# Attention with beacon keys and a low-rank mixer on one core: masks built ahead of the key loads, one q load put off, the score order of the first pair, the first mixing two blocks side by side, and the first second layer taken by halves of w2

## The chip, the core and the metric

The kernel runs on one core of one Trainium2 chip. The core has five engines that run their own instruction streams and meet through semaphores: TensorE (matrix multiply, PE in the profile; its weight loads are shown as PEld), VectorE (DVE), ScalarE (ACT), GpSimd (POOL) and SyncE (SP). Matmul results go to PSUM, which has eight banks; everything else lies in SBUF. Transfers are issued by SP, ACT or POOL and run on 16 DMA engines. The metric is the device time of the program in microseconds; a kernel's time is the median of its runs.

## The reference

Per batch (8) and head (8), causal attention over 576 tokens of width 64 with 16 beacon keys ahead of them, which every query sees. The eight heads side by side give x (576 x 512). Then a mixer: u = x + (U V applied along the tokens, rank 32), and out = u + relu(u w_ch1) w_ch2 with 512 -> 2048 -> 512.

```python
k_all = np.concatenate([beacon_k, k], axis=2)
v_all = np.concatenate([beacon_v, v], axis=2)
scores = scale * np.matmul(q, k_all.transpose(0, 1, 3, 2))
scores = np.where(causal, -1000000000.0, scores)
a = np.exp(scores - scores.max(-1, keepdims=True))
a /= a.sum(-1, keepdims=True) + 1e-09
x = np.matmul(a, v_all)                 # heads side by side
h = x.transpose(0, 2, 1) @ U @ V
u = x + h.transpose(0, 2, 1)
out = u + np.maximum(u @ w_ch1, 0.0) @ w_ch2
```

## The kernel before

**Tiling.** A pair is two heads (four pairs for each batch; pair p belongs to batch p // 4). Keys with beacons are cut into five tiles of 128 (the last shorter), queries likewise. The scores of a pair are computed with the keys on the partitions, in four groups of a PSUM bank each (`groups`; group g starts with key tile g), for both heads: 8 matmul results. ACT takes the exponential of each into `expt`, VectorE clears the masked part there (`mask_head`, L324, L326), and the weighted sums (`av_unit`, L397) use `expt` as the stationary side against v with a column of ones, so that the sum of weights comes out beside the result. For pairs 0, 1 and 4 the mask is instead added to the scores on TensorE before the exponential (`early`, L340), from `negmask`.

**Operands.** q and k of a pair are loaded with tokens on partitions, regrouped so that two heads lie side by side (`regroup`, L268, and L270 for the beacons), turned by TensorE (L275; L281 where nothing was regrouped) and copied to qT and kT (L308, L313). For pair 0 and for the q of pair 1 the loads stand in float32 in `first` (tiles `stk`, `stq`), issued by SP and ACT in `load_first` (L203); all other loads are issued by POOL, which casts to float16 in the transfer. Of pairs 0 and 1 regrouping is also the cast: for pair 0 one half is done by VectorE and the other by ACT.

**Constants.** `build_masks` makes the identity, `mask`, `bigmask` and `negmask` on POOL and VectorE. `small_loads` brings U and V (L167 to L172); its `cast` writes Usb and Vsb on POOL (L176, L177) and then copies V into the other partition groups of `Vsb` and `Vend` by transfers on SP (L181, L182). w_ch1 is loaded in four pieces (`emit_w1`, L189), w_ch2 in two halves (`emit_w2`, L195), all by POOL, between the loads of batch 0 and 1 and ahead of those of batch 2 (`load_batch(2)`).

**The order of the work.** It is written out by hand: within each engine instructions run in the order in which the program issues them. `queue` holds units of the mixer's two layers: `g_unit(dc)` is four matmuls of the first layer (L534) and a relu on ACT or VectorE (L547, L549); `c_unit(i, part)` is a quarter (four of 16 slices of the hidden width, L560) of output tile i of 128 rows. After part 3 u is added, the tile is copied to `ob` (L573 for later blocks; for the first block u is added on TensorE, L568, and the copy is VectorE's for even i, L577, and ACT's for odd i, L575) and stored by SP (L579). `fill(n)` takes n units out of the queue, and "f" in the lines of `play` is one. "q5" and "k5" turn q and k of pair 5, "r7" regroups, "v8:01" computes groups 0 and 1 of pair 8 (`visit`, L382), "a" and "b" are the two weighted sums.

Batch 0 is mixed in two halves of two 128-wide blocks each (`first_mix`): `head` multiplies U with x (L489), `begin` turns x onto PSUM (L413), `rest` adds the product with V (L506) and copies to uT. Batch 1 is mixed by `mix_units` (L434 to L476), whose pieces stand between units of the queue. After that come the lines

```python
        mix(1)
        fill(8)
        regroup_of(NP1)
        regroup_of(NP1 + 1)
        fill(8)
        play("q8 f k8 f v8:01 f q9 f k9 f r10 v8:23,9:0 f")
```

with NP1 = 8, so that the first operands of batch 2 are regrouped amid units of the first block's second layer. These are held in the order of `for i ... for part`. The queue at `mix(1)` is: the head, one unit, `most`, three units, `end`, and then units with empty places between, up to four of them; so the first `fill(8)` plays the head, units 0 to 3 with `most` and `end`, and unit 4; the second plays units 5 to 8.

PSUM banks are handed out in the order in which the program releases them (`pst`, `emptying`).

Of the kernel before, what the change touches and what calls it, by code (L numbers as in the profile page):

```python
# [11 lines left out]
F32 = mybir.dt.float32  # L12
# [6 lines left out]
P = 128  # L19
F16_MAX = 65504.0  # L20
# [10 lines left out]
def kernel(  # L31
# [13 lines left out]
    nc = tc.nc  # L45
# [76 lines left out]
    def build_masks():  # L122
        make_identity(nc, ident)
        nc.vector.memset(bigmask[:, 0, P - Nb : P], F16_MAX)
        nc.vector.tensor_copy(out=identb, in_=ident)
        token_load(nc.gpsimd, k[0], Ls[0][0][0], SETS[1])
        make_upper_triangular(nc, mask, val=F16_MAX, diag=True)
        prs[0] = [None, regroup(first, 0, 1, V, act_copy)]
        nc.vector.tensor_copy(out=bigmask[:, 0, 0 : P - Nb], in_=mask[:, Nb:P])
        nc.vector.tensor_copy(out=bigmask[:, 1, :], in_=mask)  # L130
        for i in range(2):
            nc.vector.tensor_scalar(
                out=negmask[:, i, :], in0=bigmask[:, i, :], scalar1=1.0, scalar2=NEG,
                op0=ALU.is_lt, op1=ALU.mult,
            )

    def clear():
        for c in range(2, 4):
# [23 lines left out]
    def small_loads():  # L162

        f = utp.tile([P, NT * R + S], F32, name="small", tag="ut")
        nc.vector.memset(f[0:1, 0:1], 0.0)
        uf, vf = f[:, 0 : NT * R].rearrange("p (j r) -> p j r", r=R), f[0:R, NT * R :]
        nc.sync.dma_start(out=uf[: nq[0], 0, :], in_=moe_U[0 : nq[0], :])  # L167
        nc.sync.dma_start(
            out=uf[:, 1 : NT - 1, :], in_=moe_U[q0[1] : QM, :].rearrange("(j p) r -> p j r", p=P)
        )  # L170
        nc.sync.dma_start(out=uf[:NL, NT - 1, :], in_=moe_U[QM:S, :])
        nc.sync.dma_start(out=vf, in_=moe_V)  # L172

        def cast():
            for rr, jj in ((nq[0], slice(0, 1)), (P, slice(1, NT - 1)), (NL, slice(NT - 1, NT))):
                nc.gpsimd.tensor_copy(out=Usb[:rr, jj, :], in_=uf[:rr, jj, :])  # L176
            nc.gpsimd.tensor_copy(out=Vsb[0:R, :], in_=vf)  # L177
            for cc in range(NCC):
                rs = ds(R * cc, R)
                if cc:  # L180
                    nc.sync.dma_start(out=Vsb[rs, :], in_=Vsb[0:R, :])  # L181
                nc.sync.dma_start(out=Vend[rs, cc, :], in_=Vsb[0:R, QM:S])  # L182

        return cast

# [16 lines left out]
    def token_load(eng, src, dst, hs):  # L202
        eng.dma_start(out=dst[0:TP, hs, :], in_=src[hs].rearrange("h (p j) d -> p h (j d)", j=TJ))  # L203
# [116 lines left out]
    def score_units(c, qT, kT, ex, early=False):  # L320

        def mask_head(i):
            e4 = ex[i][:, 0:EW].rearrange("p (g w) -> p g w", w=SLOT)[:, :, 0:P]
            nc.vector.tensor_tensor(out=e4, in0=e4, in1=bigmask, op=ALU.min)  # L324
            o, n = blk[(4, 4)], nq[4]
            nc.vector.tensor_tensor(  # L326
                out=ex[i][0:n, ds(o, n)], in0=ex[i][0:n, ds(o, n)], in1=mask[0:n, 0:n], op=ALU.min
            )

        def visit(gs, idle=0, by_head=True, between=None):  # L330
            turn = [(g, i) for i in range(2) for g in gs] if by_head else [(g, i) for g in gs for i in range(2)]
# [12 lines left out]
            for g in gs:  # L344
                for ch, qa, w, o in groups[g]:
                    for i in range(2):
                        hp = slice(D * i, D * i + D)
                        nc.tensor.matmul(  # L348
                            ps[g, i][:, ds(o, w)], kT[hp, c, ds(P * ch, P)], qT[hp, c, ds(qa, w)],
                            start=not early, stop=True, skip_group_check=early,  # L350
                        )

            def exps(g, i):
                nc.scalar.activation(  # L354
                    out=ex[i][:, ds(SLOT * g, gw[g])], in_=ps[g, i][:, 0 : gw[g]], func=AF.Exp, scale=scale
                )
# [11 lines left out]
        return [  # L368
            lambda idle=0, between=None: visit([0, 1], idle, between=between),
            lambda gs=[2, 3], by_head=True: visit(gs, 0, by_head), masks, mask_head,  # L370
        ]

# [108 lines left out]
    def first_mix(xb):  # L481

        qts = outp.tile([P, DM], F16, name="qfirst", tag="ob")
        cell = {}

        def head(c0, n):
            qtp = pst([R, P * n], F32, name="qtp")
            for j in range(NT):
                nc.tensor.matmul(  # L489
                    qtp, Usb[: nq[j], j, :], xb[: nq[j], j, ds(P * c0, P * n)], start=(j == 0), stop=(j == NT - 1)  # L490
                )
            nc.vector.tensor_copy(out=qts[0:R, ds(P * c0, P * n)], in_=qtp)
            emptying(qtp)

        def begin(c0, cs, n=2):
            for cc in cs:
                cell[cc] = pst([P, QM], F32, name="ups")
                x_into(xb, cell[cc], cc, list(range(NT - 1)), 0, True)
                if cc == c0:
                    cell["end"] = pst([P, n, NL], F32, name="uend")  # L500
                x_into(xb, cell["end"][:, cc - c0, :], cc, [NT - 1], QM, cc == c0)

        def rest(c0, n, copies, end):
            for at in (0, QM):
                for i in range(n):
                    nc.tensor.matmul(  # L506
                        cell["end"][:, i, :] if at else cell[c0 + i], qts[0:R, ts(c0 + i, P)],
                        Vsb[0:R, at : S if at else QM], start=False, stop=True, skip_group_check=True,
                    )
            for cc, copy in zip(range(c0, c0 + n), copies):  # L510
                copy(out=uT[:, cc, 0:QM], in_=cell[cc])
                emptying(cell[cc])
            end(out=uT[:, ds(c0, n), QM:S], in_=cell["end"])
            emptying(cell["end"])

        return head, begin, rest

    def mlp_units(t0, n, dst, flip, turned=True, last=False):
# [35 lines left out]
        def c_unit(i, part):  # L554
            m = min(P, n - P * i)
            if part == 0:
                cps["t"] = pst([P, DM], F32, name="cps")
            ps = cps["t"]
            for dc in range(4 * part, 4 * part + 4):
                nc.tensor.matmul(  # L560
                    ps[:m, :], gT["t"][:, dc, ds(P * i, m)], w2[:, dc, :], start=(dc == 0),
# [31 lines left out]
                nc.sync.dma_start(out=dst(i, P)[:, hs], in_=ob)  # L593

        units += [lambda dc=dc: g_unit(dc) for dc in range(NDC)]
        for i in range((n + P - 1) // P):
            c = c_half if last and i == n // P - 1 else c_unit
            units += [lambda i=i, part=part, c=c: c(i, part) for part in range(4)]
        return units, g_part


# [66 lines left out]
    def load_first():  # L668

        kf = gtp.tile([P, 2, TJ * D], F32, name="stk", tag="gT")  # L670
        qf = gtp.tile([P, 4, TJ * D], F32, name="stq", tag="gT")
        first.extend([kf, qf])
        for src, dst in ((q[0], qf), (k[0], kf)):
            for eng, h in ((nc.sync, 0), (nc.scalar, 1)):
                token_load(eng, src, dst, slice(h, h + 1))
        token_load(nc.sync, q[0], qf, SETS[1])
        Ls[0] = qk_tiles()
        key_beacons(nc.gpsimd, beacon_k[0], Ls[0][0][0], ALLH)
        nc.scalar.activation(out=warm, in_=ones, func=AF.Exp)
# [128 lines left out]
    with tc.manual_schedule(engines={ENG.PE, ENG.Activation, ENG.DVE, ENG.SP, ENG.Pool}):  # L808
# [11 lines left out]
        t0[0]()  # L820
        idle(IDLE[4], ident)
        t0[1]()
        sc[0](IDLE[1])
        prs[1] = [None, regroup(first, 1, 1, V)]
        for u in qkT_of(1)[::-1]:
            u()
        clear()
        cast = small_loads()
# [50 lines left out]
        rest(0, 2, (act_copy, act_copy), act_copy)  # L879
        av = av_of(3)  # L880
        av[0]()
        av[1]()
        begin(2, (2,))
        part(D0, 2)
        part(D1, 2)
        head(2, 2)
# [230 lines left out]
```

## Time and profile before

| | us |
|---|---|
| median of 3 runs | 350.42 (349.91 to 350.76) |
| profiled execution, device time | 350.22 |
| its span, first to last instruction | 348.6 |
| TensorE busy | 341.6 (98%) |
| VectorE busy | 190.5 (55%) |
| ACT busy | 163.5 (47%) |
| POOL busy | 98.0 (28%) |

All times in the views are counted from the start of the span. A row of a timeline has start, duration, engine, source line, operation, output and inputs, shape, the number of like instructions merged into it and, in brackets, how long the engine sat idle before it and what ended that. A matmul's end is modelled, so starts are the better measure of TensorE. A row of the chain of waits has start, length and the work that the end was waiting for at that time. A row of windows has the stretch, its length, the busy time and count of PE, PEld, DVE, ACT and POOL, the granted TensorE clock as a share of full speed, the DMA share and the bytes moved in GB/s. A row of DMA issues has output and input, queue, count, KB each and the median time from issue to landing. "SPq" and "POOLq" are the engines' instruction queues, where transfers are issued.

### The profile page before, as it was taken

How to read it: one execution, taken by the hardware profiler on the slowest of the kernel's cores; microseconds unless marked ns; L12 is line 12 of the kernel's file. 1: busy time of each engine (PE TensorE's matmuls, PEld its weight loads, DVE VectorE, ACT ScalarE, POOL GpSimd, SP SyncE). 2: the span in 40 equal slices, each digit the busy share in tenths (PEclk: the TensorE clock that was granted, in tenths of full speed). 3: DMA queues.
4: the chain of work that ended last, by engine and by line, in shares of the span. 5: the costliest groups of instructions: out<-in, count | busy, mean ns of one | idle time of the engine just before them, and what ended most of it. 6: DMA issues, size and time to landing. Idle time of an engine off the chain costs nothing.

```text
span 348.6 us, 7792 instructions
## 1 busy us (share of the span) xinstructions
PE 341.6 (98%) x3084; PEld 173.0 (50%) x3084; DVE 190.5 (55%) x492; ACT 163.5 (47%) x358; POOL 98.0 (28%) x137
## 2 busy tenths in 40 slices
PE   8999999999999999999999999999999999999995
PEld 3565564555554455444554545445445444444443
DVE  5776964789875653654565456535655542323311
ACT  5957851578823665167614753494434203302300
POOL 8885713653505547303830140000000000000000
PEclk9999999999999999999999999999999999999999
DMA  9999999999999999991999799613123314013011
GB/s 168 128 181 182 157 196 181 222 145 144 131 147 144 159 152 127 172 190 8 141 134 192 124 107 132 179 44 68 63 75 47 68 63 120 2 60 105 17 65 65
DMA packets 146635, 41.88 MB, mean 120 GB/s; under 512 B 131488, under 2 KB 142080, under 8 KB 146592
## 3 DMA queue, kind: packets, MB, share of 16 engines
q0 software_dynamic: 87440, 18.18, 71.6%
q1 hardware_dynamic: 58928, 22.84, 36.3%
q8 instruction: 26, 0.43, 0.6%
q10 hardware_dynamic: 224, 0.30, 0.3%
q14 instruction: 17, 0.14, 0.2%
HBM read 37.37 MB, written 9.44 MB: 134 GB/s over the span
## 4 chain that ended last, share of the span: by engine, by line
PE 88%; DMA 7%; DVE 2%; ACT 1%; issue 0%; POOL 0%
PE gps L534 35%; PE cps L560 33%; PE po L397 8%; PE sps L382 6%; DMA st<-in_q_dram 6%; ACT expt L354 1%; PE tps L275 1%; PE sps L348 1%; PE cph L586 1%; DMA stq<-in_q_dram 1%; PE qtp L434 1%; PE tps L281 1%; DVE qT L308 1%; DVE pr L268 1%; PE ups L459 1%; DVE kT L308 0%
## 5 line engine op out<-in xcount | busy, mean ns | idle before, releaser
L534 PE MATMUL gps<-uT,w 128*128 128x512 f16 x576 | 136.0, 379 | 0.1
L560 PE MATMUL cps<-w,gT 128*128 128x512 f16 x560 | 130.9, 379 | 0.1
L388 ACT ACTIVATE expt<-sps 128x496 f16<-128x496 f32 x192 | 82.5, 534 | 71.6 <-PE sps L382 71.6
L547 ACT ACTIVATE gT<-gps 128x512 f16<-128x512 f32 x86 | 50.9, 622 | 78.8 <-PE gps L534 78.7
L534 PEld LDWEIGHTS <-w 128*128 128x128 f16 x576 | 51.8, 98 | 58.0 <-issue 2.4
L560 PEld LDWEIGHTS <-gT 128*128 128x128 f16 x560 | 50.9, 98 | 59.4 <-issue 6.5
L549 DVE TENSOR_SCALAR gT<-gps 128x512 f16<-128x512 f32 x58 | 39.9, 690 | 41.6 <-PE gps L534 39.9
L573 DVE TENSOR_TENSOR ob<-cps,ut 128x512 f32<-128x512 f32 x31 | 21.4, 691 | 48.3 <-PE cps L560 47.5
L218 POOL DMA_DIRECT2D vs<-in_v_dram x50 | 39.6, 807 | 17.0 <-PE po L397 4.8
L397 PEld LDWEIGHTS <-expt 128*128 128x128 f16 (+1 forms) x960 | 36.2, 98 | 12.8 <-issue 1.0
L397 PE MATMUL po<-vs,expt 128*128 128x65 f16 (+1 forms) x960 | 38.9, 194 | 0.1
L406 DVE TENSOR_TENSOR xb<-po,rec 128x320 f16<-128x320 f32 x64 | 31.5, 491 | 2.2
L324 DVE TENSOR_TENSOR expt<-expt,bigmask 128x512 f16<-128x512 f16 x58 | 24.3, 418 | 6.7 <-ACT expt L388 6.7
L354 ACT ACTIVATE expt<-sps 128x496 f16<-128x496 f32 (+1 forms) x64 | 27.0, 606 | 0.7 <-PE sps L348 0.6
L405 DVE RECIPROCAL rec<-po 128x5 f32<-128x5 f32 x64 | 12.1, 188 | 26.9 <-PE po L397 26.6
L382 PE MATMUL sps<-qT,kT 64*128 64x80 f16 (+4 forms) x288 | 23.3, 281 | 0.1
L200 POOL DMA_DIRECT2D vs<-in_beacon_v_dram x8 | 4.3, 536 | 57.2 <-PE po L397 57.2
L646 POOL DMA_DIRECT2D st<-in_q_dram x20 | 16.9, 863 | 7.2 <-DMA vs<-in_v_dram 4.3
L382 PEld LDWEIGHTS <-kT 64*128 64x128 f16 x288 | 9.8, 94 | 18.3 <-issue 14.4
L646 POOL DMA_DIRECT2D st<-in_k_dram x20 | 16.9, 868 | 3.3 <-DMA st<-in_q_dram 2.9
L446 DVE TENSOR_TENSOR uT<-ups,uT 128x496 f16<-128x496 f32 x24 | 14.5, 667 | 5.0 <-PE ups L459 5.0
L308 DVE COPY qT<-tps 128x576 f16<-128x576 f16 (+1 forms) x16 | 11.8, 735 | 3.5 <-PE tps L281 2.3
(97 smaller groups left out, 162.4 us busy)
## 6 DMA issues: line engine op xcount, KB each, us to landing
out_dram<-ob SPq DMA_DIRECT2D x35, 256.0 KB, 2.3
vs<-in_v_dram POOLq DMA_DIRECT2D x18, 128.0 KB, 7.3
w<-in_moe_w_ch_dram POOLq DMA_DIRECT2D x4, 512.0 KB, 6.9
w<-in_moe_w_ch_dram POOLq DMA_DIRECT2D x2, 1024.0 KB, 14.3
st<-in_k_dram POOLq DMA_DIRECT2D x12, 128.0 KB, 8.9
st<-in_q_dram POOLq DMA_DIRECT2D x12, 128.0 KB, 9.4
st<-in_k_dram POOLq DMA_DIRECT2D x2, 576.0 KB, 13.1
st<-in_q_dram POOLq DMA_DIRECT2D x2, 576.0 KB, 15.9
```

Of the source, the lines that this page charges most:

```text
L218: nc.gpsimd.dma_start(out=dst[a : a + nq[j], j, :, :], in_=src[hs, ds(q0[j], nq[j]), :].rearrange("h p d -> p h d"))
L324: nc.vector.tensor_tensor(out=e4, in0=e4, in1=bigmask, op=ALU.min)
L354: nc.scalar.activation(out=ex[i][:, ds(SLOT * g, gw[g])], in_=ps[g, i][:, 0 : gw[g]], func=AF.Exp, scale=scale)
L382: nc.tensor.matmul(ps[p, g, i][:, ds(o, w)], kT[hp, c, ds(P * ch, P)], qT[hp, c, ds(qa, w)], start=True, stop=True,)
L388: nc.scalar.activation(out=at[p][3][i][:, ds(SLOT * g, gw[g])], in_=ps[p, g, i][:, 0 : gw[g]], func=AF.Exp, scale=scale)
L397: nc.tensor.matmul(po[:, j, :], ex[0 : nk[c], ds(blk[(c, j)], P)], vs[0 : nk[c], ds(c * H * E + h * E, E)], start=(c == 0), stop=(c == j),)
L406: nc.vector.tensor_tensor(out=xb[:, :, ds(h * D, D)], in0=po[:, :, 0:D], in1=r.broadcast_to([P, NT, D]), op=ALU.mult)
L534: nc.tensor.matmul(g[:, 0:n], w1[:, cc, ts(dc, P)], uT[:, cc, ds(t0, n)], start=(cc == 0), stop=(cc == NCC - 1))
L547: nc.scalar.activation(out=gT["t"][:, dc, 0:n], in_=g[:, 0:n], func=AF.Relu)
L549: nc.vector.tensor_scalar_max(out=gT["t"][:, dc, 0:n], in0=g[:, 0:n], scalar1=0.0)
L560: nc.tensor.matmul(ps[:m, :], gT["t"][:, dc, ds(P * i, m)], w2[:, dc, :], start=(dc == 0), stop=turned and dc == NDC - 1, skip_group_check ...
L646: nc.gpsimd.dma_start(out=dst[a : m[j], j, :, :], in_=src[:, ds(q0[j], nq[j]), :].rearrange("h p d -> p h d"))
```

## The change

- `build_masks`: the upper triangle and the masks made of it are issued ahead of the regrouping of the first q on VectorE, and on POOL ahead of the load of k of pair 1. The load of q of pair 1 (SP) moves from `load_first` to here, behind a one-element memset of its tile on VectorE.
- First scores: pair 0 visits group 1 ahead of group 0 (`gs=[1, 0]`).
- Pair 1: q is turned first, then k.
- `small_loads`: V is loaded twice, to partitions 0 to 31 and 32 to 63; POOL casts both to Vsb and writes the first two slices of Vend; the transfers on SP remain for the other two.
- `first_mix.head`: the two blocks go to partitions 0 to 31 and 32 to 63 of the result by the position of the tile in the array; ten matmuls of 128 columns in place of five of 256. `rest` takes the end of the tokens through Vend with both blocks as the contraction.
- One `begin` of the second half stands between the two weighted sums of pair 3.
- `mlp_units`: in the first block (`not turned and n == 512`) the first eight second-layer units are ordered (0,0), (0,1), (1,0), (1,1), (0,2), (0,3), (1,2), (1,3), so that the first four use the first half of w2; each output tile has its own entry in `cps`.

```diff
@@ build_masks
         nc.vector.tensor_copy(out=identb, in_=ident)
+        nc.vector.memset(first[1][0:1, 2, 0:1], 0.0)
+        token_load(nc.sync, q[0], first[1], SETS[1])
+        make_upper_triangular(nc, mask, val=F16_MAX, diag=True)
         token_load(nc.gpsimd, k[0], Ls[0][0][0], SETS[1])
-        make_upper_triangular(nc, mask, val=F16_MAX, diag=True)
-        prs[0] = [None, regroup(first, 0, 1, V, act_copy)]
         nc.vector.tensor_copy(out=bigmask[:, 0, 0 : P - Nb], in_=mask[:, Nb:P])
         nc.vector.tensor_copy(out=bigmask[:, 1, :], in_=mask)
...
+        prs[0] = [None, regroup(first, 0, 1, V, act_copy)]
@@ small_loads
-        nc.sync.dma_start(out=vf, in_=moe_V)
+        for i in range(2):
+            nc.sync.dma_start(out=vf[ds(R * i, R), :], in_=moe_V)
...
-            nc.gpsimd.tensor_copy(out=Vsb[0:R, :], in_=vf)
+            nc.gpsimd.tensor_copy(out=Vsb[0 : 2 * R, :], in_=vf)
             for cc in range(NCC):
                 rs = ds(R * cc, R)
-                if cc:
+                if cc > 1:
                     nc.sync.dma_start(out=Vsb[rs, :], in_=Vsb[0:R, :])
-                nc.sync.dma_start(out=Vend[rs, cc, :], in_=Vsb[0:R, QM:S])
+                    nc.sync.dma_start(out=Vend[rs, cc, :], in_=Vsb[0:R, QM:S])
+                else:
+                    nc.gpsimd.tensor_copy(out=Vend[rs, cc, :], in_=vf[rs, QM:S])
@@ first_mix
-            qtp = pst([R, P * n], F32, name="qtp")
+            qtp = pst([R * n, P], F32, name="qtp")
             for j in range(NT):
-                nc.tensor.matmul(
-                    qtp, Usb[: nq[j], j, :], xb[: nq[j], j, ds(P * c0, P * n)], start=(j == 0), stop=(j == NT - 1)
-                )
-            nc.vector.tensor_copy(out=qts[0:R, ds(P * c0, P * n)], in_=qtp)
+                for i in range(n):
+                    nc.tensor.matmul(
+                        qtp[ds(R * i, R), :], Usb[: nq[j], j, :], xb[: nq[j], j, ts(c0 + i, P)],
+                        start=(j == 0), stop=(j == NT - 1), skip_group_check=True, tile_position=(0, R * i),
+                    )
+            nc.vector.tensor_copy(out=qts[0 : R * n, ts(c0, P)], in_=qtp)
...
-            for at in (0, QM):
-                for i in range(n):
-                    nc.tensor.matmul(
-                        cell["end"][:, i, :] if at else cell[c0 + i], qts[0:R, ts(c0 + i, P)],
-                        Vsb[0:R, at : S if at else QM], start=False, stop=True, skip_group_check=True,
-                    )
+            for i in range(n):
+                nc.tensor.matmul(
+                    cell[c0 + i], qts[ds(R * i, R), ts(c0, P)], Vsb[ds(R * i, R), 0:QM],
+                    start=False, stop=True, skip_group_check=True,
+                )
+            for i in range(n):
+                nc.tensor.matmul(
+                    cell["end"][:, i, :], qts[0 : R * n, ts(c0, P)], Vend[0 : R * n, i, :],
+                    start=False, stop=True, skip_group_check=True,
+                )
@@ mlp_units
-        for i in range((n + P - 1) // P):
+        turns = [(i, part) for i in range((n + P - 1) // P) for part in range(4)]
+        if not turned and n == 512:
+            turns[0:8] = [(i, part) for h in (0, 2) for i in (0, 1) for part in (h, h + 1)]
+        for i, part in turns:
             c = c_half if last and i == n // P - 1 else c_unit
-            units += [lambda i=i, part=part, c=c: c(i, part) for part in range(4)]
+            units.append(lambda i=i, part=part, c=c: c(i, part))
@@ load_first
-        token_load(nc.sync, q[0], qf, SETS[1])
@@ the order of the work
-        sc[0](IDLE[1])
+        sc[0](IDLE[1], gs=[1, 0])
         prs[1] = [None, regroup(first, 1, 1, V)]
-        for u in qkT_of(1)[::-1]:
+        for u in qkT_of(1):
...
         av[0]()
+        begin(2, (2,))
         av[1]()
-        begin(2, (2,))
```

More of the change, by code (lines that the diff above doesn't have):

```diff
@@ L165, in small_loads @@
         nc.vector.memset(f[0:1, 0:1], 0.0)
[L166 removed]
+        uf, vf = f[:, 0 : NT * R].rearrange("p (j r) -> p j r", r=R), f[0 : 2 * R, NT * R :]
         nc.sync.dma_start(out=uf[: nq[0], 0, :], in_=moe_U[0 : nq[0], :])
@@ L368, in score_units @@
         return [
-            lambda idle=0, between=None: visit([0, 1], idle, between=between),
+            lambda idle=0, between=None, gs=[0, 1]: visit(gs, idle, between=between),
             lambda gs=[2, 3], by_head=True: visit(gs, 0, by_head), masks, mask_head,
@@ L556, in c_unit @@
             if part == 0:
-                cps["t"] = pst([P, DM], F32, name="cps")
-            ps = cps["t"]
+                cps[i] = pst([P, DM], F32, name="cps")
+            ps = cps[i]
             for dc in range(4 * part, 4 * part + 4):
```

## The prediction

> **What bounds the kernel now.** I read the page first, then the chain of waits, then the stretch that the chain names, in order of time.
>
> ```profile
> PE 341.6 (98%) x3084; PEld 173.0 (50%) x3084; DVE 190.5 (55%) x492; ACT 163.5 (47%) x358; POOL 98.0 (28%) x137
> PE 88%; DMA 7%; DVE 2%; ACT 1%; issue 0%; POOL 0%
> ```
>
> TensorE is busy for 341.6 of 348.6 us, so it looks as if everything saved on TensorE were a gain. The 7% of DMA in the chain says otherwise for the first 60 us, where the whole change lies. The chain, in order of time:
>
> ```profile
> 38.90 20.70 DMA st<-in_q_dram
> 59.63 0.62 DVE pr L268 x2
> 60.27 0.40 DVE pr L270
> 60.70 0.36 DVE pr L268
> 61.05 0.67 DVE qT L308
> 61.72 0.68 DVE kT L308
> 62.53 0.58 PE sps L382 x4
> ```
>
> The load of q of batch 2 is issued at 38.90, stands in a queue, and lands 20.70 us later, at 59.6. Then VectorE regroups (L268, L270) and copies the turned q and k (L308) without a gap until 62.4, and the scores of pair 8 start at 62.53. From there to the end the chain is TensorE alone. TensorE around that place:
>
> ```profile
> 59.02 1.03 PE L560 MATMUL cps<-w,gT 128*128 128x512 f16 x4
> 60.04 0.43 PE L275 MATMUL tps<-ident,pr 96*128 96x96 f16 x6
> 60.31 1.03 PE L560 MATMUL cps<-w,gT 128*128 128x512 f16 x4
> 61.17 0.43 PE L275 MATMUL tps<-ident,pr 96*128 96x96 f16 x6
> 61.44 1.03 PE L560 MATMUL cps<-w,gT 128*128 128x512 f16 x4
> ```
>
> Four matmuls from 60.31 take 0.86 until the next start at 61.17; the four from 59.02 take 1.02, so 0.16 us of it is waiting; the four from 61.44 take 1.09, up to 0.23 of it waiting. TensorE thus reaches this place just before the data. What it gains earlier it waits away here; what delays q's landing, or VectorE's chain behind it, moves the end.
>
> **Start and mixing: TensorE comes earlier.** The mask work now stands ahead of the first casts on VectorE.
>
> ```profile
> 1.79 0.43 SPq L203 DMA_DIRECT2D stq<-in_q_dram  x1
> 2.73 0.25 DVE L125 CAST identb<-ident 128x128 bf16<-128x128 f16 x1 [0.76 <-POOL ident masks.py:199]
> 4.18 0.55 DVE L268 CAST pr<-stq 96x384 f16<-96x384 f32 x1 [1.20 <-DMA stq<-in_q_dram]
> 5.02 0.52 ACT L682 ACTIVATE pr<-stk 96x384 f16<-96x384 f32 x1 [0.32 <-DMA stk<-in_k_dram]
> 5.25 0.54 DVE L268 CAST pr<-stk 96x384 f16<-96x384 f32 x1
> 7.34 13.22 ACT L354 ACTIVATE expt<-sps 128x496 f16<-128x496 f32 x32 [0.63 <-PE sps L348]
> ```
>
> The masks move into the 1.20 us of waiting before 4.18, and VectorE's half of the key cast starts with ACT's, at 5.02 and not 5.25: 0.23 us earlier to the first scores and to the 32 exponentials that now start at 7.34. The new order of the scores (key tile 1 first) keeps the same matmuls and the same four exponentials. The second pair's q load leaves 1.79 and waits on SP for a VectorE memset behind the cast that ends at 2.98, so it goes some 1.2 us later; only the small loads of U and V are queued behind it on SP, much later. VectorE still reads it near 6.5, so I take nothing, bounds 0 and 0.3 off the 0.23. That pair's k load goes on POOL behind the two mask instructions and is read later than before, behind q's: nothing.
>
> ```profile
> 18.81 0.72 PE L489 MATMUL qtp<-xb,Usb 112*32 112x256 f16 x5
> 49.29 0.61 PE L434 MATMUL qtp<-xb,Usb 112*32 112x128 f16 x20
> 52.01 2.98 PE L560 MATMUL cps<-w,gT 128*128 128x512 f16 x12
> 55.35 3.62 PE L560 MATMUL cps<-w,gT 128*128 128x512 f16 x16
> ```
>
> Each of the two heads goes from five matmuls of 256 columns to ten of 128 in two column groups. Twenty in four groups, the later mixing's form, take 0.61, so ten take no more: 0.11 saved at least; halving 0.72 gives 0.36 at most. I take 0.2 for each head, 0.4 in all. The K=64 matmuls in `rest` keep their columns, and `begin(2, (2,))` moves ahead of `av[1]` as it is, so nothing. Sixteen second-layer matmuls take 3.62, so twelve would take 3.62 less 4 of 0.215 (0.86 / 4), 2.76; the 2.98 has 0.22 of waiting in it, where the third unit first needs w2's second half. Four units that read the first half alone now come first, so that wait goes. Sum of TensorE's lead at q8: 0.23 + 0.4 + 0.22 = 0.85, bounds 0.4 (the heads' 0.11, q 0.3 late) and 1.2. By itself this is worth 0: the cover is the load that lands at 59.6, and if that were gone it would be worth the whole 0.85.
>
> The Trainium skill, TensorEngine Tiling (Array Packing), section Theoretical Speedup, says that a stationary side of at most 32 columns may run up to four tiles at once. By that rule two side by side halve each head and the lead is 1.2, by the x20 row as a bound 0.7; the forecast's sum is the same by both, but the fastest rival below would end near 349.2 by the rule and near 349.7 by the row.
>
> **The second layer's new order: VectorE comes later.** Before, unit (0,3) ends the first output tile ahead of `end` of mix(1), and its copy runs here:
>
> ```profile
> 55.26 0.69 DVE L577 COPY ob<-cps 128x512 f32<-128x512 f32 x1 [1.86 <-PE cps L568]
> 55.86 0.48 DVE L448 CAST uT<-uend 128x320 f16<-128x320 f32 x1
> 59.63 0.62 DVE L268 COPY pr<-st 96x768 f16<-96x768 f16 x2 [2.80 <-DMA st<-in_q_dram]
> ```
>
> Now the queue plays (0,0), (0,1), (1,0), (1,1), `end`, (0,2), then the code's `regroup_of(8)` and `regroup_of(9)`, then (0,3), (1,2), (1,3). VectorE takes its work in order, so the copy of the first output tile stands behind both regroups, that is behind q's landing, and ahead of the copies of qT and kT at 61.05. VectorE had 2.80 us of waiting behind the old place of this copy; now the copy lies in the gapless chain that releases the scores. Its step there is 0.60 (55.26 to 55.86). So the scores of pair 8 wait 0.60 us more, and TensorE, which has spent its two units between, has nothing else to issue. Bounds: 0 if the chain is not what releases the scores, 0.69 by the full duration. I take 0.60. The bank that the copy empties late is next taken by the fourth score tile of that visit, later in any case. (1,3) is copied on ACT, which waits for nothing here.
>
> **When q lands.** It stands at the end of POOL's issue order, so every earlier queue step counts.
>
> ```profile
> 14.01 0.81 POOL L189 DMA_DIRECT2D w<-in_moe_w_ch_dram  x1
> 16.11 0.53 POOL L176 CAST Usb<-small 128x96 f16<-128x96 f32 x2 [1.07 <-DMA small<-in_moe_U_dram]
> 16.68 0.66 POOL L177 CAST Vsb<-small 32x576 f16<-32x576 f32 x1
> 17.30 0.69 POOL L203 DMA_DIRECT2D st<-in_k_dram  x1
> 31.51 3.58 POOL L218 DMA_DIRECT2D vs<-in_v_dram  x5 [1.37 <-DMA st<-in_q_dram]
> 13.00:15.00 2.00, 1.85 (x36) 1.06 (x37) 1.32 (x6) 2.00 (x6) 2.00 (x4) 1.00 1.89 164
> 15.50:16.50 1.00, 0.79 (x27) 0.60 (x21) 1.00 (x4) 1.00 (x5) 0.34 (x2) 1.00 0.78 57
> 19.00:20.00 1.00, 1.00 (x22) 0.76 (x21) 0.96 (x4) 1.00 (x5) 1.00 (x3) 1.00 1.06 156
> 37.50:57.00 19.50, 19.31 (x231) 10.79 (x231) 13.88 (x40) 10.43 (x24) 7.15 (x11) 1.00 1.24 193
> Vsb<-Vsb SPq DMA_DIRECT2D x3, 36.0 KB, 6.2
> Vend<-Vsb SPq DMA_DIRECT2D x4, 5.0 KB, 5.6
> small<-in_moe_V_dram SPq DMA_DIRECT2D x1, 72.0 KB, 5.2
> w<-in_moe_w_ch_dram POOLq DMA_DIRECT2D x4, 512.0 KB, 6.9
> ```
>
> In the four rows of windows the last two columns are DMA share and GB/s, in those of DMA issues KB each and us to landing. POOL issues without a wait up to 14.01, and the masks only swap places there, so that part keeps its times. Then three things change.
> - V is loaded twice: 72 KB more. At 164 GB/s (the stretch in which it moves) that is 0.45 us of queue; the dip to 57 GB/s just behind can hold it. Bounds 0 and 0.45, taken 0.1.
> - One copy Vsb to Vsb and two to Vend leave SP's queue, 46 KB with 5 KB for each of the latter: 0.28 us at 164 GB/s. Bounds -0.28 and 0, taken -0.1.
> - POOL casts two more slices to Vend, each about 0.25 (the 128x96 pair above is 0.53), and its Vsb cast waits for V's second half, 0 to 0.45 later. What is queued behind on POOL is the load of k of batch 1 at 17.30 and all after it, now 0.5 to 0.95 later. At 19 to 20 the share is 1.06 against 1.24 in the full stretch, so the queue is then nearly empty, and a late k leaves a hole. Bounds 0 and 0.95; the first w1 piece, issued at 14.01, is still landing then (6.9 us, to 20.9), which covers most of the hole, so 0.2.
>
> Sum 0.1 - 0.1 + 0.2 = 0.2, bounds -0.3 and 1.4. At 31.51 POOL itself waits for a landing, so such a shift goes on to 59.6.
>
> The Trainium skill, DMA: Bandwidth & Descriptors, section Rules for kernel authors, says that loads issued from several engines run on the same 16 DMA engines and interleave. By that rule V's second load takes queue time from the k and v loads though SP issues it; at the 435 GB/s that the page's Specifications give for the fabric it would be an estimated 0.17 us, at the row's 164 GB/s 0.45, the upper bound above.
>
> **The sum.** Span 348.6, and 1.62 around it make the profiled execution's 350.22, 0.20 under the median of 350.42. Added: 0 (TensorE's lead) + 0.60 (copy) + 0.2 (landing) = 0.8, so 351.0 against that execution and 351.2 against the median.
>
> **The rivals.** 0.2% is 0.70 us, about what a measurement of this kernel tells from none: 349.72 to 351.12 counts as the same.
> - Forecast, 351.2, own range 350.9 to 351.6, chance 0.42.
> - The landing does not move or comes 0.3 earlier, the copy still costs 0.6: 350.7 to 351.0, taken 350.9. For it: the dip at 15.5 and the copies that leave. Against it: the casts on POOL. Chance 0.26.
> - A hole in the queue: the k load of batch 1 is a full 0.95 late and V's load costs 0.45; with the copy, 350.42 + 0.60 + 0.95 + 0.45 - 0.28 is 352.1; it decides from a landing 0.7 later. For it: share 1.06 at 19 to 20. Against it: the w1 piece that is still landing. Chance 0.17.
> - Faster: TensorE's 0.85 carries through, 349.6. The mechanism is an earlier q: from 0.6 earlier the added copy costs nothing, from 1.45 earlier the whole lead counts. For it: only 0.28 of DMA work is removed, but the queue has holes of its own (57 GB/s at 15.5) that loads issued a little earlier could fill. Chance 0.15.
>
> The likeliest gives 351.2. Faster takes 0.14 of the last case; the same takes the second case but 0.02, 0.13 of the first and 0.01 of the last; slower the rest: 0.14, 0.38, 0.48. The range reaches down to the faster rival and up to the hole: 349.6 to 352.1.
>
> **What would show it.** Right: the first exponential near 7.1 and not 7.34; no wait among the first second-layer units; TensorE waiting about 1.2 us at the first transposes of pair 8; the L577 copy after the four regroup copies, ahead of qT; q landing between 59.6 and 60.2; the first k load of batch 1 issued near 18. Wrong: q landing before 59.0, or scores of pair 8 starting before 62.5.

## The result, and the profile after

| | before | after |
|---|---|---|
| median of 17 runs each, us | 350.48 (349.73 to 352.21) | 351.97 (350.61 to 353.62) |
| ratio after to before, 95% | | 1.0047 (1.0034 to 1.0060) |
| profiled execution, its span | 348.6 | 349.8 |
| TensorE busy in it | 341.6 | 341.9 |

The changed kernel is slower: by 1.49 us by the medians, by 1.65 by the ratio (0.0047 of 350.5). Its profiled execution took 351.5 us, 1.3 more than the one of before (350.22).

The chain of waits after, in order of time (start, length, what the end was waiting for), has a stretch that the chain of before did not have, from 11.88 to 25.90:

```profile
11.88 5.36 DMA small<-in_moe_V_dram
17.36 0.83 POOL Vsb L180
...
18.70 1.29 POOL st L208 x2
19.98 5.87 DMA st<-in_beacon_k_dram
25.90 0.50 PE tps L286 x14
...
39.54 20.51 DMA st<-in_q_dram
60.07 0.62 DVE pr L273 x2
...
61.49 0.60 DVE ob L588
62.09 0.66 DVE qT L313
62.76 0.66 DVE kT L313
63.55 0.58 PE sps L387 x4
```

There are two places to read. The second load of V lands at 17.24; POOL's cast waits for it, the loads of batch 1 queue behind that cast, and the beacon keys of batch 1 land at 25.86, where TensorE waits for them. Later q of batch 2 lands at 60.05 in place of 59.60, and the copy of the first output tile (L588, formerly L577) stands between the regroups and the copy of qT, for 0.60. From the first regroup to the scores of pair 8 it was 2.90 us (59.63 to 62.53) and is 3.48 (60.07 to 63.55). The scores start 1.02 later: 0.44 from the landing, 0.58 from the copy.

POOL's timeline after, at the first place:

```profile
16.15 0.42 POOL L179 CAST Usb<-small 128x96 f16<-128x96 f32 x2 [1.09 <-DMA small<-in_moe_U_dram]
17.36 0.83 POOL L180 CAST Vsb<-small 64x576 f16<-64x576 f32 x1 [0.79 <-DMA small<-in_moe_V_dram]
18.15 0.55 POOL L187 CAST Vend<-small 32x80 f16<-32x80 f32 x2
18.65 0.68 POOL L208 DMA_DIRECT2D st<-in_k_dram  x1
```

The first k load of batch 1 leaves at 18.65 and not 17.30, 1.35 later. The V cast starts 0.68 later (17.36 against 16.68); the rest is that it lasts longer and is followed by two more casts. TensorE's timeline at the turns of pair 4, after and then before:

```profile
24.84 0.40 PE L286 MATMUL tps<-ident,st 96*64 96x96 f16 x10
25.90 0.50 PE L286 MATMUL tps<-ident,st 112*64 112x112 f16 x14 [0.65 <-DMA st<-in_beacon_k_dram]
26.33 1.04 PE L545 MATMUL gps<-uT,w 128*128 128x512 f16 x4
```

```profile
25.33 0.71 PE L281 MATMUL tps<-ident,st 96*64 96x96 f16 x24
25.98 1.25 PE L534 MATMUL gps<-uT,w 128*128 128x512 f16 x5
```

Before, the 24 transposes ran from 25.33 without a stop and the first layer went on at 25.98. Now they begin 0.49 earlier, stop after ten, and the first layer goes on at 26.33: a lead of 0.49 became a lag of 0.35. TensorE's timeline after, at the first head, in the second layer and at pair 8:

```profile
19.02 0.46 PE L495 MATMUL qtp<-xb,Usb 112*32 112x128 f16 x10
...
52.42 2.77 PE L571 MATMUL cps<-w,gT 128*128 128x512 f16 x12
...
59.21 1.03 PE L571 MATMUL cps<-w,gT 128*128 128x512 f16 x4
60.49 0.43 PE L280 MATMUL tps<-ident,pr 96*128 96x96 f16 x6 [0.25 <-DVE pr L273]
...
61.88 1.03 PE L571 MATMUL cps<-w,gT 128*128 128x512 f16 x4
63.55 0.58 PE L387 MATMUL sps<-qT,kT 64*128 64x496 f16 x4 [0.64 <-DVE kT L318]
```

The head takes 0.46 (before 0.72), and the twelve second-layer matmuls 2.77 (before 2.98): no wait for w2's second half is left. At pair 8 TensorE waits twice. Four matmuls start at 59.21 and the turns at 60.49, 0.42 after the 0.86 that the four take; four more start at 61.88 and the scores at 63.55, 0.80 after them. The two make 1.22, near the 1.2 that was forecast for the turns alone, but not as a lead waited away: TensorE starts the last four matmuls ahead of the turns at 59.21, where it started them at 59.02 before. The wait comes from the late landing and the copy.

One more step follows, at the regroup of pair 11. The timeline after (POOL, VectorE, TensorE), and below it that of before (VectorE, TensorE):

```profile
74.20 4.21 POOL L660 DMA_DIRECT2D st<-in_k_dram  x5 [4.05 <-DMA st<-in_q_dram]
76.16 0.67 DVE L275 COPY pr<-st 16x128 f16<-16x128 f16 x1
77.86 0.42 PE L280 MATMUL tps<-ident,pr 96*128 96x96 f16 x6
```

```profile
75.13 0.47 DVE L270 COPY pr<-st 16x128 f16<-16x128 f16 x1
76.65 0.42 PE L275 MATMUL tps<-ident,pr 96*128 96x96 f16 x6
```

The turns of pair 11 start 1.21 later, 0.19 more than the scores of pair 8; the copy of the beacons ahead of them took 0.20 longer. From there to the end both kernels run alike, and the spans differ by 1.2.

### The profile page after: what moved, and what is told of

Same layout as the page of the kernel before. It is cut to its first block, busy times and chain, and to the rows that moved or that the text cites. A ratio compares the mean times of both kernels' runs of the same rounds, so it can differ in the third digit from the quotient of the medians.

```text
span 349.8 us, 7813 instructions
## 1 busy us (share of the span) xinstructions
PE 341.9 (98%) x3094; PEld 173.3 (50%) x3094; DVE 190.4 (54%) x493; ACT 163.6 (47%) x358; POOL 98.2 (28%) x139
## 4 chain that ended last, share of the span: by engine, by line
PE 87%; DMA 9%; DVE 2%; POOL 1%; SPq 0%; issue 0%; POOLq 0%
PE gps L545 34%; PE cps L571 32%; PE po L402 7%; PE sps L387 6%; DMA st<-in_q_dram 6%; DMA st<-in_beacon_k_dram 2%; DMA small<-in_moe_V_dram 2%; PE tps L280 1%; PE idle L255 1%; PE cph L597 1%; PE sps L353 1%; PE qtp L439 1%; PE ups L464 1%; PE tps L286 1%; DVE qT L313 0%; DVE kT L313 0%
## 5 line engine op out<-in xcount | busy, mean ns | idle before, releaser
L359 ACT ACTIVATE expt<-sps 128x496 f16<-128x496 f32 (+2 forms) x64 | 27.0, 612 | 1.0 <-PE sps L353 1.0
```

Of the source, the lines that this page charges most:

```text
L359: nc.scalar.activation(out=ex[i][:, ds(SLOT * g, gw[g])], in_=ps[g, i][:, 0 : gw[g]], func=AF.Exp, scale=scale)
```

## The experiments

The theory: two costs, the late load of k of batch 1 (a term that the prediction made too small) and the copy in VectorE's chain. The main rival: the added time lies elsewhere, in the new matmuls or the start. Times are medians; each ratio is to the kernel before on the same chip, with its 95% interval, and 0.001 is 0.35 us.

**1. The changed kernel with the second-layer units in the old order.**

```diff
-        if not turned and n == 512:
-            turns[0:8] = [(i, part) for h in (0, 2) for i in (0, 1) for part in (h, h + 1)]
```

> The changed kernel with the second layer's units of the first block in their old order, all else as changed. Theory A (the change costs 0.60 us through the copy that stands behind both regroups, and the rest through the late loads of batch 1 behind POOL's casts): the L577-type copy runs before the regroup copies again, scores of pair 8 start 0.6 us earlier against q's landing, and the median falls by 0.4 to 0.7 us, to 351.3 to 351.6. Rival B (the order of the units costs nothing; the later start and the late loads cost all): 351.9 to 352.0, as the changed kernel.

Measured: 351.20, ratio 1.0011 (0.9996 to 1.0026). Most of the loss goes, though in its profile the stall at pair 4 is still there (turns at 25.82). That execution shows more: its first k load of batch 1 left at 18.45, 1.15 later than before, and yet VectorE's first regroup of pair 8 started at 59.33, 0.30 earlier than before, and the span was 348.5. No cost of the late load or of the stall is seen there.

**2. The changed kernel with the loads and casts of V and the first mixing as before.**

```diff
-        for i in range(2):
-            nc.sync.dma_start(out=vf[ds(R * i, R), :], in_=moe_V)
+        nc.sync.dma_start(out=vf, in_=moe_V)
...
-                else:
-                    nc.gpsimd.tensor_copy(out=Vend[rs, cc, :], in_=vf[rs, QM:S])
```

> The changed kernel with V's loads, POOL's casts and the first mixing as before. Theory A: POOL issues the first k load of batch 1 near 17.3 and not 18.65, its beacon load lands near 24.8 and not 25.9, the 0.8 us wait of TensorE at the turns of pair 4 goes, q of batch 2 lands near 59.6 and not 60.05; what is left is the copy, so about 0.6 us over before, 351.0 to 351.2. Rival B (the start, with scores 0.18 us later, and the order of the loads there cost it): 351.7 to 352.0.

Measured: 350.82, ratio 1.0012 (0.9991 to 1.0034). Taking out this part also gives most of it back. Two parts of which either gives back some 1.2 of 1.65 do not simply add.

**3. The changed kernel with POOL's casts behind the first three loads of batch 1.**

```diff
-        cast()
         Ls[1] = qk_tiles()
...
         key_beacons(nc.gpsimd, beacon_k[1], kt, ALLH)
+        cast()
```

> The changed kernel with POOL's casts of U and V issued behind the first loads of k, q and beacon k of batch 1 and not ahead of them. Theory A: those loads are issued from 14.9 on, the dip of the queue at 15.5 and 19 closes, they land 2 us or more earlier, TensorE does not wait at the turns of pair 4, and q of batch 2 lands 0.3 to 1 us earlier; the copy's 0.6 stays: 350.4 to 351.1. Rival C (the queue up to q of batch 2 is bound by its packets alone, holes are filled by slow engines): q lands as in the changed kernel near 60.0 and the time stays within 0.3 us of 352.0.

Measured: 350.68, ratio 0.9998 (0.9985 to 1.0011): no loss that can be told is left, with every other part of the change in place. POOL's timeline of this kernel:

```profile
15.14 0.68 POOL L208 DMA_DIRECT2D st<-in_k_dram  x1
16.31 0.67 POOL L208 DMA_DIRECT2D st<-in_q_dram  x1 [0.48 <-DMA st<-in_q_dram]
...
18.63 0.74 POOL L187 CAST Vend<-small 32x80 f16<-32x80 f32 x2
```

The k load leaves at 15.14, 3.5 earlier than in the changed kernel, and q of batch 2 lands at 58.37. VectorE copies the output tile before TensorE has turned q, and the copy delays nothing:

```profile
59.46 0.36 DVE L273 COPY pr<-st 96x768 f16<-96x768 f16 x1
59.74 0.68 DVE L588 COPY ob<-cps 128x512 f32<-128x512 f32 x1
60.51 0.76 DVE L313 COPY qT<-tps 128x576 f16<-128x576 f16 x1
61.64 0.76 DVE L313 COPY kT<-tps 128x576 f16<-128x576 f16 x1 [0.37 <-PE tps L280]
```

Ahead of the copy of kT VectorE is idle for 0.37, waiting for TensorE's turn: TensorE is last here. The k load leaves 2.16 earlier than even in the kernel before, so this run shows that the loss needs q's landing to be last; it does not show what the delay of 1.35 costs by itself.

**4. The kernel before with the new unit order alone** (the `mlp_units` part of the diff).

> The kernel before with the new order of the second layer's first eight units alone. Theory A: 0.60 us slower than before (351.0 to 351.2): q of batch 2 lands as before at 59.6, the copy lies between the regroup copies and those of qT. Rival B (the order only removes the 0.22 us wait for w2's second half): 350.2 to 350.5.

Measured: 350.83, ratio 1.0009 (0.9997 to 1.0021): 0.3 with an interval that takes in zero and 0.6. Its profile shows the copy's step (from the first regroup at 59.73 to the scores at 63.22 it is 3.49). It also bears on pair 4. No load was touched, the k load left at 17.31, and TensorE stopped there all the same:

```profile
26.58 0.50 PE L281 MATMUL tps<-ident,st 112*64 112x112 f16 x14 [0.76 <-DMA st<-in_beacon_k_dram]
```

**5. The kernel before with a late load alone**, made by casting V three times.

```diff
-            nc.gpsimd.tensor_copy(out=Vsb[0:R, :], in_=vf)
+            for _ in range(3):
+                nc.gpsimd.tensor_copy(out=Vsb[0:R, :], in_=vf)
```

> The kernel before; POOL casts V three times in place of once (0.66 us each), so the first k load of batch 1 is issued 1.32 us later (18.6, not 17.30) and nothing else of the change is in. Theory (the late load is the mis-sized term: it stalls TensorE at pair 4's transposes, near 25.9, and moves q of batch 2 by about 0.4): 350.9 to 351.1 against 350.5 before. Rival (the queue fills the hole, as the prediction took it; only 0.2 of such a delay arrives): 350.5 to 350.7.

Measured: 351.92, ratio 1.0036 (1.0021 to 1.0051): 1.3, above what either theory said. Its chain of waits:

```profile
17.10 0.67 POOL Vsb L178
...
19.27 1.30 POOL st L204 x2
...
40.89 20.37 DMA st<-in_q_dram
61.29 0.62 DVE pr L269 x2
```

In this execution the k load left 1.93 later than before (19.23), 0.42 of it because the V cast itself started later, and q of batch 2 landed at 61.26, 1.66 later. So a delay of this size can arrive almost whole 40 us on. The edit has a side effect: TensorE's first head waits 0.39 for POOL's casts.

**6. Late load and new order together, without the start and the mixing** (the edits of 4 and 5).

> The same late load together with the new order of the second-layer units, without the start's and the mixing's edits. Theory (late load and displaced copy add, since the chain from q's landing to the scores of pair 8 has no slack: 0.4 and 0.6, and TensorE's lead is eaten at pair 4): 351.5 to 352.0, most of what the whole change costs. Rival (each costs what it costs alone, 0.35 for the units and what the late load shows, and the rest of the change's 1.5 lies in the mixing's matmuls or the start): at most 351.2.

Measured: 352.50, ratio 1.0049 (1.0029 to 1.0069). These two edits alone cost as much as the whole change. Its chain shows both terms:

```profile
40.71 20.75 DMA st<-in_q_dram
61.49 0.62 DVE pr L269 x2
...
62.91 0.60 DVE ob L578
63.51 0.67 DVE qT L309
...
64.97 0.58 PE sps L383 x4
```

The landing is 1.86 later than before, and from the first regroup to the scores it is 3.48, as in the changed kernel.

**7. The changed kernel with the copy of the first output tile on ACT.** The edit also moves one copy of a later path that is not executed here.

```diff
-                elif i % 2:
+                elif i % 2 or (n == 512 and i == 0):
```

> The changed kernel; the first output tile's copy is done by ACT in place of VectorE, so it leaves the chain from q's landing to the scores of pair 8, and all else stays. Theory (the copy costs its 0.60 step there): 0.6 less than the changed kernel, 351.3 to 351.5, and in the profile qT's copy starts 0.6 earlier after the regroups. Rival (the chain is not what releases the scores, or the first exponentials behind ACT's copy take it back): 351.9 to 352.1.

Measured: 351.87, ratio 1.0030 (1.0016 to 1.0043), against 1.0047: a gain of about 0.6 by the ratios, but they are from two chips and their intervals overlap. In this execution V's second half landed only at 18.82, the k load left at 20.25, and TensorE was last at pair 8; the copy's step could not be seen.

**8. The kernel before with the first mixing's edits alone** (`small_loads`, `first_mix`, the moved `begin`).

> The kernel before with the first mixing's edits alone: V loaded twice, two slices cast by POOL, the two blocks side by side. Theory (its price is the late load, 1.35 as in the changed kernel; the heads' 0.4 come back as waiting at pair 4's transposes): 350.9 to 351.1, as with the late load alone, and a stall near 25.9. Rival (the side-by-side matmuls' gain carries through): 350.0 to 350.3.

Measured: 351.17, ratio 1.0015 (1.0000 to 1.0031). In the range of the late load, not of a gain. In its profile V landed early (16.46), the k load left 0.61 later than before, TensorE stopped for 0.52 at the turns of pair 4, q landed 0.40 earlier than before, and the span was 348.7.

**9. The kernel before with half the delay** (V cast twice).

> The kernel before with V cast twice by POOL in place of once: the first k load of batch 1 is issued 0.66 us later (near 17.96), a delay inside the 0.5 to 0.95 that the prediction allowed, which it priced at 0.2. Theory (such a delay arrives nearly whole at the landing of q of batch 2, since each later load starts behind it on POOL; three casts cost 1.3): 351.0 to 351.3 against 350.5 to 350.6 before. Rival (a threshold: the queue and TensorE's lead take a delay of this size, as the prediction had it): 350.5 to 350.8.

Measured: 350.70, ratio 1.0011 (0.9990 to 1.0031). The middle is 0.4, but the interval holds both answers: whether a delay of 0.66 is free stays open.

**10. The kernel before with its casts behind the first three loads of batch 1** (the edit of 3).

> The kernel before with POOL's casts of U and V put behind the first k, q and beacon loads of batch 1, nothing else. The k load is issued near 14.9 in place of 17.30. Theory (the landing of q of batch 2 follows the k load, here 0.8 to 1.2 earlier, and TensorE's lead of about 0.4 at pair 8 then counts): 350.0 to 350.3, a gain of 0.3 to 0.5. Rival (the later landing was only a matter of this kernel's delays; an earlier one is worth nothing since TensorE sets the end then): 350.4 to 350.6; over 350.8 if the later casts hold up the first mixing.

Measured: 350.39, ratio 0.9993 (0.9982 to 1.0005). No gain that can be told. Its scores of pair 8 start at 62.51 (before 62.53) though q lands 0.76 earlier: TensorE is last. An earlier load was worth nothing here; the rival was right.

**11. The changed kernel with the old order and late casts** (the edits of 1 and 3).

> The changed kernel with the second-layer units in the old order and POOL's casts behind the first three loads of batch 1. Theory (both costs gone, and what the start and the mixing give TensorE can count): 349.9 to 350.4, at or under the kernel before. Rival (the copy was no cost, so this equals the changed kernel with its casts late, or TensorE sets the end either way): 350.5 to 350.8.

Measured: 350.54, ratio 0.9997 (0.9979 to 1.0015). Like experiment 3 and like the kernel before, as the rival had it. No version beat the kernel before by more than the measurement can tell.

**12. The kernel before with the start's edits alone.**

> The kernel before with the start's edits alone: masks ahead of the key casts, q of pair 1 issued later, key tile 1 scored first, q of pair 1 turned before k. The loads of batch 1 keep their place behind the same casts. Theory (the cost of the change lies in the late load and the copy, none of it here): 350.3 to 350.7, within 0.2 of the kernel before. Rival (part of the missing time is the start's, which came 0.18 later to its scores in the changed kernel): 350.8 to 351.1.

Measured: median 351.28 (the kernel before on this chip 350.63), but ratio 0.9998 (0.9973 to 1.0023). The spread within the kernel (350.21 to 353.14) is too wide to say more than that nothing of 1.65 is shown to lie here. The profiled execution, the longest of them, shows one source of spread, a row of TensorE's timeline and one of windows:

```profile
15.49 0.70 PE L283 MATMUL tps<-ident,st 96*64 96x96 f16 x12 [1.48 <-DMA st<-in_k_dram]
16.00:18.00 2.00, 2.00 (x37) 1.49 (x32) 1.26 (x3) 1.42 (x4) 1.58 (x5) 0.50 1.03 127
```

TensorE waits 1.48 for a k load of batch 0, and from 16 to 22 its granted clock is 0.50, where the kernel before has 1.00.

**13 to 15. The changed kernel, its old order and its copy on ACT on one chip.** Experiments 1 and 7 had come from different chips; these are the same kernels side by side, with 16.

> The changed kernel itself, beside the three below on one chip: 351.6 to 352.2 (351.97 when it was first timed), 1.2 to 1.7 over the kernel before.

> The changed kernel with the second-layer units in their old order. Theory (the order costs its copy, 0.60, where q's landing sets the end): 0.5 to 0.8 under the changed kernel of this call. Rival (the order costs more than its copy, as the 1.26 of the two chips says): 1.0 to 1.4 under it, and clearly under the one with the copy on ACT.

> The changed kernel with the first output tile's copy on ACT. Theory: 0.4 to 0.7 under the changed kernel of this call, and within 0.3 of the old order's time. Rival: 0 to 0.3 under the changed kernel, 0.8 or more over the old order's time.

Measured: the changed kernel 351.38, ratio 1.0018 (1.0004 to 1.0031); the old order 351.17, ratio 1.0013 (0.9994 to 1.0032); the copy on ACT 351.50, ratio 1.0024 (1.0008 to 1.0039). All three expectations were missed: here the change costs 0.6 by the ratio (0.8 by the medians) and not 1.65, and the three cannot be told apart. So neither of the two prices of the new order (0.6 or 1.2) is shown in the medians. The profiles do show the copy's step. The chain with the copy on ACT:

```profile
39.51 20.46 DMA st<-in_q_dram
59.99 0.62 DVE pr L273 x2
...
61.41 0.67 DVE qT L313
...
62.89 0.58 PE sps L387 x4
```

It is 2.90 from the first regroup to the scores, as before the change, where the changed kernel and experiment 6 have 3.48. With the old order on this chip another wait ended last ahead of pair 8, the one that the new order was seen to remove: a load of w2, issued at 36.93, landed at 53.06, and the second-layer matmuls went on at 53.10.

**16. The changed kernel with the two end slices of V copied by transfers again.**

```diff
-                    nc.sync.dma_start(out=Vend[rs, cc, :], in_=Vsb[0:R, QM:S])
-                else:
-                    nc.gpsimd.tensor_copy(out=Vend[rs, cc, :], in_=vf[rs, QM:S])
+                nc.sync.dma_start(out=Vend[rs, cc, :], in_=Vsb[0:R, QM:S])
```

> The changed kernel with the two end slices of V copied by transfers from SP again in place of POOL's casts; V is still loaded twice. The first k load of batch 1 leaves 0.55 earlier, near 18.1. Theory (each part of the delay counts, the casts with their 0.55 of 1.35): 0.4 to 0.7 under the changed kernel of this call. Rival (the wait for V's second half is what costs, or the delay counts only as a whole): within 0.2 of the changed kernel.

Measured: 354.70, ratio 1.0110 (1.0077 to 1.0144), a miss of both. TensorE's timeline of this kernel shows the larger part of the reason:

```profile
21.64 0.19 PE L515 MATMUL uend<-Vend,qfirst 64*128 64x80 f16 x1 [0.94 <-DMA Vend<-Vsb]
23.82 0.19 PE L515 MATMUL uend<-Vend,qfirst 64*128 64x80 f16 x1 [1.98 <-DMA Vend<-Vsb]
```

The new `rest` reads both slices near 20.7, and the transfers land up to 23.8. The two waits make 2.9 of the 3.9 that the ratio gives. Behind them the granted clock of the profile is 0.76 from 24 to 26, 0.50 to 28 and 0.88 to 30, where the kernel before has 1.00: by these figures an estimated 1.7 more of TensorE's time. That is more than 3.9 together, so not all of it reached the end. Before, `rest` read Vsb, and these copies were needed only near 55. The two casts on POOL were the price of the new form, and the split of the late load into casts and wait was not settled by this run.

## Why the prediction was right or wrong

**Direction and chain: right.** The time went to the named place: q of batch 2 (landing at 60.05, inside the 59.6 to 60.2 that were named), VectorE's regroups and copies with L577's copy among them, the scores of pair 8.

**The copy, 0.60: right as a step.** It measured 0.60 in the chain and 0.58 from the first regroup to the scores. That the landing must be last for it to count is shown by experiment 3.

**The k load of batch 1: the step that failed.** The prediction bounded the delay by 0.5 to 0.95 and took 0.2 of it to arrive at q's landing, since "the first w1 piece, issued at 14.01, is still landing then". The delay was 1.35, outside the bounds: V's second half held the cast back by 0.68 (bound 0.45), and POOL's casts from there took 0.67 longer (0.5 was counted; in this execution the wider V cast took 0.83 in place of 0.66). And q landed 0.44 later, more than twice the 0.2: the w1 piece did not cover the rest. That each later load stands behind this one in POOL's order would explain it; it was argued, not tried.

How much of a delay arrives differs between executions. Against the kernel before, in the profiles with the casts ahead of the loads:

| run | k load leaves later by | first regroup of pair 8 starts later by |
|---|---|---|
| experiment 8 | 0.61 | -0.41 |
| experiment 9 | 0.74 | -0.26 |
| experiment 14 | 0.88 | -0.47 |
| experiment 15 | 0.96 | 0.36 |
| experiment 1 | 1.15 | -0.30 |
| the changed kernel | 1.35 | 0.44 |
| experiment 6 | 1.81 | 1.86 |
| experiment 13 | 1.87 | 1.01 |
| experiment 5 | 1.93 | 1.66 |
| experiment 7 | 2.95 | 0.64 |

From 1.35 on the landing is late each time; up to 1.15 it is early in four of five, so a delay inside the prediction's bounds cannot be told from the scatter of landings. One execution of each is too little for a threshold, and experiment 13 (the changed kernel again, in an execution of 354.16, the longest of its 14) shows how far two executions of one program lie apart. By the medians experiment 5 shows that a delay of 1.3 or more alone costs 1.3, and experiment 9 leaves open whether half of it is free.

This is the rival "a hole in the queue", which had 0.17 and 352.1. Its sign, a landing 0.7 later, was there in experiment 13 and not in the profile after (0.44). That its 352.1 is near the measured 351.97 is luck: its terms beside the copy make 1.12, where the profile has 0.63.

**TensorE's lead, 0.85, worth nothing: right in the end, wrong on the way.** The heads gave 0.52 for the two (0.4 taken; 0.26 each lies between the bounds 0.11 and 0.36), the twelve matmuls took 2.77 (2.76 worked out). The start gave no lead in this execution: the scores start at 7.12 and not 6.94 and the first exponential at 7.52, not near 7.1, for a reason told below. And the lead was not waited away at pair 8 but at pair 4, for the beacon keys of batch 1. The prediction followed the late load to q of batch 2 alone and never asked which of TensorE's operands in between are issued behind it. That the late issue made the stop at pair 4 is not shown, though: experiment 4 stops there for 0.76 with its loads on time, and experiments 5 and 13, with the k load 1.9 late, do not stop, as TensorE comes there some 0.55 later than before.

**The sum.** In the profile: 0.44 for the landing, 0.58 for the copy and 0.19 at pair 11, which was not foreseen: 1.2 against the 0.8 of the sum. The first timing gave 1.65, that of experiment 13 gave 0.6, with intervals that barely miss each other. The lowest single runs differ by less: 350.61 against 349.73, and 350.51 against 349.86 on the second chip, 0.9 and 0.65. So the mis-sized term of the profile is the landing, and what else is in the median of the first timing stays open. That it is the scatter of landings, which the changed kernel feels more, having less slack at pair 8, was argued from the spreads and not tried by itself.

## What to carry to other kernels

When an edit puts work on an engine that also issues loads, price the delay of every load behind it, and follow each to its first reader, not only to the one that ends the chain now. Do not count on a busy DMA queue to cover a late issue: here a delay of 1.35 or more was seen again at a load that lands 40 us on, and only smaller ones were lost in the scatter. And where a copy moves behind a load on an in-order engine, its full step counts as soon as that load is last.

## What the runs showed of the hardware

**The first microseconds of TensorE differ from run to run.** The same matmul of 128x512 in the start, first after and then before:

```profile
5.06 0.63 PE L255 MATMUL idle<-ident 128*128 128x512 f16 x1
```

```profile
5.05 0.38 PE L250 MATMUL idle<-ident 128*128 128x512 f16 x1
```

It takes 0.63 against 0.38, six turns 0.69 against 0.43, though the view of windows gives a granted clock of 1.00 from 3.7 to 7 for both. In experiment 12, with the same start as the changed kernel, it took 0.38 and the scores began at 6.67. The Trainium skill, TensorE: Matmul & The Clock Gate, part 1, says that the array starts at half rate and that the length of this phase differs from run to run, as its window runs freely; the durations of these rows agree, the granted clock of the windows does not show it.

**VectorE's copies stretch while POOL issues transfers.** The copy of 16x128 took 0.19 at the least and up to 0.69 in the profile after; the 0.67 at 76.16 fell into POOL's issues from 74.20 to 78.4, and the 0.47 of before at 75.13 into issues from 72.94 to 76.3. The Trainium skill, SBUF — State Buffer, section Who interferes with whom, says that a copy in a two-port mode and GpSimd lock each other out of a shared port. The rows fit that rule; no run here tried it by itself.

**Two waits of TensorE were followed by a low clock.** In experiment 12 a wait of 1.48 was followed by a granted clock of 0.50 from 16 to 22, and there fifteen matmuls of 128x65 took 1.01 in place of 0.63; in experiment 16 waits of 0.94 and 1.98, close together, were followed by 0.50 from 26 to 28. Waits of 1.02 to 1.39 in the profiles of experiments 7, 9 and 13 were not followed by it (1.00 from 7 to 31), and no run here tried what decides it.

**A landing moves by a microsecond or more between runs.** V's second half landed at 17.24, 17.74 and 18.82 in three executions with the same loads ahead of it. An experiment that changes the issue of a load by less than that needs more runs than were made here (experiment 9).
